# Gated attention and a gelu layer on one core: narrower scores for the last chunk, Strassen products in every batch, and a rearranged start

## The chip, the cores and the metric

The kernel runs on one core of a Trainium2 chip. The metric is the device time of one execution in microseconds (us). A timed run gives one number. The profile is the hardware's record of one execution: for the kernel before it is one more execution beside the timed ones. "Span" is the time from the first to the last instruction of that record; it is some 2 us below the run's device time.

TensorE is PE, its weight loads PEld, VectorE DVE, ScalarE ACT, GpSimd POOL, SyncE SP. PSUM is the memory in which PE leaves its results; ACT or DVE must copy a bank of it out ("drain" it) before PE may use it again.

## The reference, cut to what matters

```python
# u, v: 8 x 3008 x 256, z: 8 x 3008 x 64
scores = (1 / S) * z @ z.T                    # per batch, S = 3008
attn   = maximum(scores, 0) ** 2
x      = u * (attn @ v)                       # 24064 x 256
h      = x @ w_in                             # 256 x 2048
g      = h / (1 + exp(-1.702 * h))
out    = g @ w_out                            # 2048 x 256
```

## The kernel before: the parts that matter

A batch has 3008 rows: five chunks of 512 queries and a last one of 448. 3008 is 23 blocks of 128 and one of 64, and those 64 rows stand twice in the last key block (partitions 0-63 and 64-127). A score unit `(i, jp)` is two key blocks against one chunk of queries. Its two matmuls have 64 rows each and run beside each other in the two halves of the array. ACT then takes the relu, DVE squares it. Because the score matrix is symmetric, squared units of chunk `i` are transposed by DMA (`turn_unit`) and serve later chunks; "turned" units of earlier chunks take over work of the last chunk.

```python
def scores(b, group):                                   # 512 columns always
    ...
        m = CB // 2 if folded(b, i) and jp == 2 * i + 1 else CB
        for r in range(2):
            pe.matmul(sc[:, r, :m * P], zt[h, 2 * kp + r, :],
                      zt[h, (qi + 1) * CB - m:(qi + 1) * CB, :], start=True, stop=True)
```

The second layer's right side `g @ w_out` is made by seven Strassen products (Strassen's method multiplies matrices of 2 x 2 blocks with seven block products, P1 to P7, instead of eight) per chunk of 512 rows (two pairs of row blocks), each product 2 x 8 matmuls of 128 columns. Batches go in pairs: the last chunk of an even batch has 384 rows and that of the odd one 512, which include both 64-row remainders. The 384 rows (three blocks) were made by plain matmuls of 256 columns:

```python
def down(b, k, s):                                      # even batches, last chunk, s = 0, 1, 2
    for ff in range(NFF):                               # 16
        pe.matmul(yp[:, s % 2, :], GT[b, k, ff // CB][:, ff % CB, s * P:(s + 1) * P],
                  W2[:, ff, :], ...)                    # 256 columns
```

At the start of batch 0, z comes in six groups of 512 rows. DVE casts each group to 16 bits, twice (two halves of the same tile), PE transposes it, and ACT or DVE copies it from PSUM to `ZT`. V comes in f32 and POOL casts it. Emission order is the order of each engine's queue:

```python
first_z(0, CB, sp); first_z(CB, 2 * CB, act)            # z groups 0, 1
for n0 in (0, VB): load_v(0, n0)                        # V; its second half chunk on ACT's queue
first_z(2 * CB, 4 * CB, act)                            # z groups 2, 3
...
posts = scores(0, [queue.pop(0) for _ in range(2)])
first_cast(2)                                           # DVE: z group 2
for post_ in posts: post_()                             # ACT relu, DVE square of units 0, 1
keep_warm(3); posts = scores(0, [queue.pop(0)]); keep_warm(2)
first_zt(2)()                                           # PE transposes z group 2
posts[0]()                                              # third unit's relu and square
```

## Time and profile before

| | before |
|---|---|
| median of 3 runs | 1193.93 us (1193.65 to 1197.71) |
| profiled run, span | 1192.27 us, 1190.5 us |
| PE, ACT, DVE busy | 99%, 70%, 69% of the span |

From the page: the busy line and the chain of waits.

```profile
PE 1184.3 (99%) x11433; PEld 721.7 (61%) x11433; DVE 823.6 (69%) x1321; ACT 828.5 (70%) x982; POOL 230.9 (19%) x325
...
PE 98%; DVE 1%; DMA 0%; issue 0%; ACT 0%; ACTq 0%
```

PE is the limit: it is on the chain for 98% of the span, so only what PE does, or waits for, counts. From the groups of PE by form (busy time, mean ns of one, idle before it): the scores and the plain products.

```profile
L244 PE MATMUL sc<-ZT 64*128 64x512 f16 x618 | 111.3, 377 | 0.7
...
L542 PE MATMUL yp<-W,gt 128*128 128x256 f16 x192 | 21.6, 273 | 0.0
```

The mean of one (377 ns) is its pipelined length, not its cost. The cost is the distance to the next start. The timeline of the end of an even batch (start in us, length, engine, line, operation) shows it:

```profile
446.75 1.06 PE L486 MATMUL st<-WT,gt 128*128 128x128 f16 x16
447.64 1.06 PE L486 MATMUL st<-W,gt 128*128 128x128 f16 x16
448.54 1.06 PE L486 MATMUL st<-WT,gt 128*128 128x128 f16 x16
449.43 1.06 PE L486 MATMUL st<-W,s 128*128 128x128 f16 x16
450.32 5.40 PE L542 MATMUL yp<-W,gt 128*128 128x256 f16 x48
455.66 0.39 PE L244 MATMUL sc<-ZT 64*128 64x512 f16 x2
```

A product of 16 matmuls of 128 columns takes 0.89 us from start to start, 56 ns each. The 48 plain ones take 5.34 us, of which about 0.1 us is the change of form before the scores.

At the start DVE was the one to look at. The chain of waits in the first 12 us (start, us, what), and two lines of DVE's timeline (in brackets the idle time before and what ended it):

```profile
1.67 5.59 DMA zf<-in_z_dram
7.26 0.02 issue
7.29 0.49 DVE zst L125 x2
7.78 1.62 DVE a L272 x2
```

```profile
7.29 0.49 DVE L125 CAST zst<-zf 128x256 f16<-128x256 f32 x2 [1.34 <-DMA zf<-in_z_dram]
7.70 1.70 DVE L272 TENSOR_TENSOR a<-rl 128x1024 f16<-128x1024 f16 x2
```

DVE stood idle for 1.34 us until z group 2 landed at 7.26 us, cast it, and only then squared the first unit.

### The profile page before, as it was taken

Reading aid. Unit: us, or ns where it says so; the run is one execution under the profiler, and the core shown is the slowest. Engines: PE = TensorE matmul, PEld = TensorE weight load, DVE = VectorE, ACT = ScalarE, POOL = GpSimd, SP = SyncE. Lnnn points to the kernel's source line nnn. Section 1 sums busy time; section 2 is a strip of 40 time slices with the busy share of each in tenths; the row PEclk is TensorE's granted clock in tenths of the full one; section 3 lists DMA queues with packets and bytes.
Section 4 is the critical chain, followed back from the end, with each engine's and each line's share of the span. In section 5 each row is a group of like instructions: output and inputs, shape, how many; then the busy total and the mean of one; then the engine's idle time right before and its main releaser. Section 6 shows DMA issues by size and latency. Waiting matters only on the chain.

```text
span 1190.5 us, 27555 instructions
## 1 busy us (share of the span) xinstructions
PE 1184.3 (99%) x11433; PEld 721.7 (61%) x11433; DVE 823.6 (69%) x1321; ACT 828.5 (70%) x982; POOL 230.9 (19%) x325
## 2 busy tenths in 40 slices
PE   9999999999999999999999999999999999999998
PEld 3446765467654676546765478554775547855577
DVE  7788755777658775577765877558776487664776
ACT  6878865688656886478864787657876578672785
POOL 5243100231012320133101331014200241001000
PEclk9999999999999999999999999999999999999999
DMA  9996667766687667856778458886579755695012
GB/s 226 191 125 111 128 131 136 84 112 134 138 138 78 108 143 146 130 72 101 160 139 135 68 96 158 159 110 90 104 128 171 108 88 109 138 164 97 1 37 72
DMA packets 373037, 141.80 MB, mean 119 GB/s; under 512 B 315440, under 2 KB 366384, under 8 KB 372912
## 3 DMA queue, kind: packets, MB, share of 16 engines
q1 hardware_dynamic: 314784, 97.30, 45.3%
q0 software_dynamic: 57280, 42.03, 22.7%
q8 instruction: 89, 1.46, 0.5%
q10 hardware_dynamic: 848, 0.72, 0.2%
q14 instruction: 36, 0.29, 0.1%
HBM read 60.29 MB, written 24.64 MB: 71 GB/s over the span
## 4 chain that ended last, share of the span: by engine, by line
PE 98%; DVE 1%; DMA 0%; issue 0%; ACT 0%; ACTq 0%
PE o L344 40%; PE hg L385 27%; PE st L486 23%; PE sc L244 6%; PE yp L542 2%; DMA zf<-in_z_dram 0%; DVE a L272 0%; DVE zst L125 0%; DVE ZT L153 0%; ACT rl L258 0%; ACT ZT L151 0%; ACTq L187 0%; DVE y L502 0%; ACTq L111 0%; PE zp L143 0%
## 5 line engine op out<-in xcount | busy, mean ns | idle before, releaser
L393 ACT ACTIVATE gf<-hg 128x1024 f32<-128x1024 f32 (+1 forms) x384 | 385.5, 1004 | 138.1 <-PE hg L385 115.2
L258 ACT ACTIVATE rl<-sc 128x1024 f16<-128x1024 f32 x309 | 303.2, 1027 | 151.8 <-PE sc L244 148.5
L344 PEld LDWEIGHTS <-V 64*128 64x128 f16 (+1 forms) x4052 | 238.2, 94 | 235.8 <-issue 11.9
L385 PE MATMUL hg<-xt,W 128*128 128x512 f16 (+1 forms) x1408 | 354.6, 374 | 0.0
L397 DVE TENSOR_SCALAR gt<-gf 128x1024 f16<-128x1024 f32 (+1 forms) x320 | 222.5, 696 | 136.7 <-ACT gf L393 133.9
L344 PE MATMUL o<-a,V 64*128 64x512 f16 (+3 forms) x2286 | 303.0, 368 | 0.1
L272 DVE TENSOR_TENSOR a<-rl 128x1024 f16<-128x1024 f16 x274 | 189.8, 698 | 154.1 <-ACT rl L258 153.3
L206 POOL DMA_DIRECT2D uq<-in_u_dram x188 | 127.7, 687 | 612.9 <-PE sc L244 329.3
L344 PE MATMUL o<-tt,V 64*128 64x512 f16 (+1 forms) x1510 | 234.3, 377 | 0.0
L385 PEld LDWEIGHTS <-W 128*128 128x128 f16 x1536 | 139.3, 98 | 119.2 <-issue 2.6
L486 PEld LDWEIGHTS <-gt 128*128 128x128 f16 x2816 | 169.5, 98 | 31.9
L486 PEld LDWEIGHTS <-s 128*128 128x128 f16 x2112 | 127.8, 98 | 25.4 <-issue 0.3
L244 PE MATMUL sc<-ZT 64*128 64x512 f16 (+1 forms) x688 | 121.0, 366 | 0.7
L486 PE MATMUL st<-WT,gt 128*128 128x128 f16 x1408 | 93.0, 219 | 0.0
L486 PE MATMUL st<-WT,s 128*128 128x128 f16 x1408 | 92.3, 219 | 0.0
L486 PE MATMUL st<-W,gt 128*128 128x128 f16 x1408 | 92.3, 219 | 0.0
L502 DVE SCALAR_TENSOR_TENSOR y<-st,uP 128x256 f32<-128x256 f32 x132 | 54.9, 418 | 21.6 <-PE st L486 10.9
L395 ACT ACTIVATE gt<-gf 128x1024 f16<-128x1024 f32 (+1 forms) x64 | 65.9, 1030 | 2.1
L361 DVE TENSOR_TENSOR xt<-o,ut 128x512 f16<-128x512 f32 x80 | 51.3, 683 | 22.7 <-PE o L344 22.7
L244 PEld LDWEIGHTS <-ZT 64*128 64x128 f16 x688 | 38.9, 94 | 44.9 <-issue 9.7
L496 ACT ACTIVATE uP<-st 128x256 f32<-128x256 f32 x132 | 49.6, 376 | 23.2 <-PE st L486 11.2
L459 DVE TENSOR_TENSOR s<-s,gt 128x1024 f16<-128x1024 f16 x88 | 61.5, 699 | 1.0
(54 smaller groups left out, 620.9 us busy)
## 6 DMA issues: line engine op xcount, KB each, us to landing
out_dram<-y SPq DMA_DIRECT2D x40, 512.0 KB, 3.3
uq<-in_u_dram POOLq DMA_DIRECT2D x156, 128.0 KB, 3.7
V<-in_v_dram POOLq DMA_DIRECT2D x35, 256.0 KB, 6.6
tt<-a SPq DMA_TRANSPOSE x232, 3.7
uq<-in_u_dram POOLq DMA_DIRECT2D x32, 112.0 KB, 5.2
vst<-in_v_dram SPq DMA_DIRECT2D x4, 512.0 KB, 6.4
out_dram<-y POOLq DMA_DIRECT2D x4, 384.0 KB, 3.1
zst<-in_z_dram POOLq DMA_DIRECT2D x7, 192.0 KB, 8.4
```

The costliest lines, as they stand in the source:

```text
L206: eng.dma_start(uq[k * QW:(k + 1) * QW, :n // QW].rearrange("t q c k -> t q (c k)"), src[:, :, cs])
L244: pe.matmul(sc[:, r, :m * P], zt[h, 2 * kp + r, :], zt[h, (qi + 1) * CB - m:(qi + 1) * CB, :], start=True, stop=True,)
L258: act.activation(rl, sc, AF.Relu, scale=csc)
L272: dve.tensor_tensor(a, rl, rl, ALU.mult)
L344: ins = pe.matmul(acc[c][:, :n], V16[b][h, j].rearrange("p (c k) -> p k c", k=NCC)[:, c], weights(b, i, j)[h], start=(k, m) == first[c], s ...
L385: pe.matmul(hg[:, e, :n], W1[:, c, ff * P:(ff + 1) * P], XT[b, i][:, c, :n], start=(c == 0), stop=(c == NCC - 1),)
L393: act.activation(gf[:, :, :n], hg[:, :, :n], AF.Gelu_apprx_sigmoid, scale=1.0 / FSC)
L395: act.activation(g, gf[:, :, :n], AF.Copy, scale=FSC)
L397: dve.tensor_scalar(g, gf[:, :, :n], FSC, None, ALU.mult)
L459: dve.tensor_tensor(s_, ST[b, k, "S1", h], a11, ALU.subtract)
L486: pe.matmul(bank[:, m, :], lhs()[:, f, m, :], right[:, ff, :], start=name in ("P1", "P2", "P5") and m == 0 and ff == 0, stop=ff == NFF // ...
L502: dve.scalar_tensor_tensor(y[:, :, o, c], ST[b, k, "bank" + x], 1.0 / FSC, ST[b, k, "after" + u_], ALU.mult, ALU.add,)
```

## The change

Four parts: (1) scores whose queries are the last chunk have 448 instead of 512 columns, and a small extra square fills the repeated 64 columns of the turned units; (2) of the three row blocks that even batches left to plain matmuls, two become Strassen products of 8 matmuls and the third stays plain; (3) in batch 0 the first square no longer stands behind the cast of z group 2, whose transposition moves into the first steps; later casts come earlier; (4) batch 0's DMA transposes are issued in order of use.

```diff
@@ scores, square
-            m = CB // 2 if folded(b, i) and jp == 2 * i + 1 else CB
+            q0, q1 = qi * CH, qi * CH + width(qi)          # width: 448 in the last chunk
+            if folded(b, i) and jp == 2 * i + 1:
+                q0 += CH // 2
-                    sc[:, r, :m * P], ..., zt[h, (qi + 1) * CB - m:(qi + 1) * CB, :],
+                    sc[:, r, :q1 - q0], ..., zt[h].rearrange("d n p -> d (n p)")[:, q0:q1],
-        dve.tensor_tensor(a, rl, rl, ALU.mult)
+        dve.tensor_tensor(a[:, :, :n], rl[:, :, :n], rl[:, :, :n], ALU.mult)
+        if turn:
+            twice = rl[:, :, LFULL:LAST]
+            dve.tensor_tensor(a[:, :, LAST:], twice, twice, ALU.mult)
+            elif b == 0 and jp < NU - 2:                   # transposes in ORDER0
+                squared.setdefault((i, jp // 2), []).append(lambda: turn_unit(b, i, jp, a))
+                while ORDER0 and len(squared.get(ORDER0[0], ())) == 2:
+                    ...
@@ products of the second layer (each sum, copy and output cut to [:, :pairs(b, k)])
+        for k in range(NCH):
             one = [(k, "P6"), (k, "P5"), (k, "P7"), (k, "P2")]
+            if blocks(b)[k][1] < CH:
+                one.insert(0, (k, "odd"))                  # 16 plain matmuls of 256 columns
             lst += [(k, "P1")] + ([(k - 1, "P4"), (k - 1, "P3")] if k else []) + one
@@ start of batch 0
-    FIRST_ZT, FIRST_CAST = {11: 3, 20: 4, 29: 5}, {2: 3, 15: 4, 24: 5}
+    FIRST_ZT, FIRST_CAST = {2: 2, 11: 3, 19: 4, 28: 5}, {2: 3, 8: 4, 16: 5}
+    posts[0]()
     first_cast(2)
-    for post_ in posts:
-        post_()
+    posts[1]()
...
-    first_zt(2)()
-    posts[0]()
...
+                if (b, i, n) == (0, 0, 2):
+                    posts[0]()
```

More of the change, by code (lines that the diff above doesn't have):

```diff
@@ L244, in scores @@
                 pe.matmul(
-                    sc[:, r, :m * P], zt[h, 2 * kp + r, :], zt[h, (qi + 1) * CB - m:(qi + 1) * CB, :],
+                    sc[:, r, :q1 - q0], zt[h, 2 * kp + r, :], zt[h].rearrange("d n p -> d (n p)")[:, q0:q1],
                     start=True, stop=True,
@@ L257, in square @@
             return
-        act.activation(rl, sc, AF.Relu, scale=csc)
+        turn = turned(b, i) and jp >= NU - 2
+        n = width(NCH - 1 if turn else i)
+        act.activation(rl[:, :, :n], sc[:, :, :n], AF.Relu, scale=csc)
         if folded(b, i) and jp == 2 * i:
@@ L275, in square @@
                 late.append(((jp + 2) % NU, lambda: turn_unit(b, i, jp, a)))
+            elif b == 0 and jp < NU - 2:
+                squared.setdefault((i, jp // 2), []).append(lambda: turn_unit(b, i, jp, a))
+                while ORDER0 and len(squared.get(ORDER0[0], ())) == 2:
+                    for turn_it in squared.pop(ORDER0.pop(0)):
+                        turn_it()
             else:
                 turn_unit(b, i, jp, a)
+    ORDER0 = [(0, 1), (0, 2), (1, 2), (0, 3), (1, 3), (0, 4), (2, 3), (1, 4), (2, 4), (3, 4)]
+    squared = {}
     def turn_unit(b, i, jp, a):
@@ L399, in up_group, with pairs @@
             s_()
-        if k < nst(b) and fg in (NFG - 3, NFG - 1):
+        if fg in (NFG - 3, NFG - 1):
             SUMS.extend(left_sums(b, k, fg == NFG - 1))
-    def nst(b):
-        return NCH - 1 + b % 2
+    def pairs(b, k):
+        return blocks(b)[k][1] // (2 * P)
     SUMS, ST = [], {}
@@ L439, in left @@
         g = GT[b, k, h].rearrange("p f (m o t) -> p f m o t", o=2, t=P)
-        return g[:, :, :, odd, :]
+        return g[:, :, :pairs(b, k), odd, :]
     def left_sums(b, k, last):
@@ L454, in left_sum @@
             return
-        s_ = ST[b, k, name, h] = pa.tile([P, CB, 2, P], F16, name="s", tag="a", bufs=26)
+        s_ = pa.tile([P, CB, 2, P], F16, name="s", tag="a", bufs=26)
+        s_ = ST[b, k, name, h] = s_[:, :, :pairs(b, k)]
         if name == "S1":
@@ L461, in left_sum, with products, odd_block @@
             dve.tensor_tensor(s_, a12, ST[b, k, "S2", h], ALU.subtract)
-    def products(n):
+    def products(b):
         lst = []
-        for k in range(n):
+        for k in range(NCH):
             one = [(k, "P6"), (k, "P5"), (k, "P7"), (k, "P2")]
+            if blocks(b)[k][1] < CH:
+                one.insert(0, (k, "odd"))
             lst += [(k, "P1")] + ([(k - 1, "P4"), (k - 1, "P3")] if k else []) + one
-        return lst + [(n - 1, "P4"), (n - 1, "P3")]
+        return lst + [(k, "P4"), (k, "P3")]
+    def odd_block(b, k):
+        s = blocks(b)[k][1] // P - 1
+        yp = ps1.tile([P, D], F32, name="yp", tag="ps1")
+        for ff in range(NFF):
+            pe.matmul(
+                yp, GT[b, k, ff // CB][:, ff % CB, s * P:(s + 1) * P], W2[:, ff, :],
+                start=ff == 0, stop=ff == NFF - 1,
+            )
+        act.activation(Y[b, k][:, s, :], yp, AF.Copy, scale=1.0 / FSC)
     def product(b, k, name):
+        if name == "odd":
+            odd_block(b, k)
+            return
+        mm = pairs(b, k)
         right = {
@@ L478, in product @@
         bank = ST[b, k, "bank" + {"P6": "P1", "P7": "P1", "P4": "P1", "P3": "P5"}.get(name, name)]
-        for m in range(2):
+        for m in range(mm):
             for ff in range(NFF // 2):
@@ L492, in product @@
             Y[b, k] = pw.tile([P, CB, D], F32, name="y", tag="y")
-        y = Y[b, k].rearrange("p (m o) c -> p m o c", o=2)
+        y = Y[b, k].rearrange("p (m o) c -> p m o c", o=2)[:, :mm]
+        bank = bank[:, :mm]
         if name in ("P1", "P6", "P7"):
-            u_ = ST[b, k, "after" + name] = pw.tile([P, 2, P], F32, name="u" + name, tag="u" + name, bufs=1 + (name != "P1"))
+            u_ = pw.tile([P, 2, P], F32, name="u" + name, tag="u" + name, bufs=1 + (name != "P1"))
+            u_ = ST[b, k, "after" + name] = u_[:, :mm]
             act.activation(u_, bank, AF.Copy, scale=1.0 / FSC)
@@ L502, in product @@
             dve.scalar_tensor_tensor(
-                y[:, :, o, c], ST[b, k, "bank" + x], 1.0 / FSC, ST[b, k, "after" + u_], ALU.mult, ALU.add,
+                y[:, :, o, c], ST[b, k, "bank" + x][:, :mm], 1.0 / FSC, ST[b, k, "after" + u_], ALU.mult, ALU.add,
             )
@@ L533, in store @@
                 )
-    def down(b, k, s):
-        if s % 2 == 0:
-            ST[b, k, "yp"] = ps1.tile([P, 2, D], F32, name="yp", tag="ps1")
-        yp = ST[b, k, "yp"]
-        for ff in range(NFF):
-            pe.matmul(
-                yp[:, s % 2, :], GT[b, k, ff // CB][:, ff % CB, s * P:(s + 1) * P], W2[:, ff, :],
-                start=s % 2 == 0 and ff == 0, stop=ff == NFF - 1, skip_group_check=True,
-            )
-        last = s == blocks(b)[k][1] // P - 1
-        if s == 0:
-            Y[b, k] = pw.tile([P, CB, D], F32, name="y", tag="y")
-        if s % 2 or last:
-            act.activation(Y[b, k][:, s - s % 2:s + 1, :], yp[:, :s % 2 + 1, :], AF.Copy, scale=1.0 / FSC)
-        if last:
-            store(b, k, pool)
     LAGY = 2 * NFG
@@ L647 @@
                     load_u(0, 0)
+                if b == 0 and i == 0 and n in FIRST_ZT:
+                    first_zt(FIRST_ZT[n])()
                 if b == 0 and i == 0 and n in FIRST_CAST:
                     first_cast(FIRST_CAST[n])
-                if b == 0 and i == 0 and n in FIRST_ZT:
-                    first_zt(FIRST_ZT[n])()
                 if (i, n) in turn:
@@ L673 @@
                 load_v(b + 1, n0)
-        prods = products(nst(b))
+        prods = products(b)
         for q in range(head, nup):
@@ L684 @@
         steps = [lambda kp=kp: product(b, *kp) for kp in prods]
-        if nst(b) < NCH:
-            k = NCH - 1
-            steps += [lambda s=s: down(b, k, s) for s in range(blocks(b)[k][1] // P)]
         for step in steps:
```

## The prediction

> **What bounds the kernel now.** TensorE: busy 1184.3 of 1190.5 us (99%) in the page's busy table, DVE 69%, ACT 70%; the chain of waits is 98% PE; clock 1.00. After 30 us the timeline has only single PE stalls of about 0.2 us. So outside the start only fewer TensorE cycles count.
>
> The Trainium skill ("TensorE: Matmul & The Clock Gate", the part on 56 ns) gives a warm matmul as N / 2.4 GHz plus about 2.5 ns. The trace agrees: in the chain 176 matmuls of 128 columns took 9.83 us (55.9 ns each), 48 of 256 took 5.24 us (109.2 ns); in the timeline a pair of 64-row matmuls of 512 columns takes 0.216 us, of 448 columns 0.190 us.
>
> **Terms.**
>
> 1. 448 columns. In every batch 12 score units have the last chunk's queries: 96 of 344. Each saves 64 columns of one pair, 0.0267 us: **-2.6 us**, all on the critical path. ACT saves 0.1 us per unit, DVE gains a small square (0.2 us) in 37 units: off the path.
>
> 2. Strassen for the last chunk of the 4 even batches. Before: 48 x 109.2 ns = 5.24 us. After: 16 x 109.2 (odd block) + 56 x 55.9 = 4.87 us: -0.37 each. But products of 8 matmuls last 0.45 us, and draining a bank (ACT starts 0.2 us after the last matmul issued; 0.27 us for 128 columns, an estimate from 0.60 for 512 and 0.38 for 256) takes 0.5. So P7 (waits for P6's copy across P5) and P4 (P7's copy across P2) should stall about 0.1 us each. Net about -0.25 each: **-1.0 us**. The half-size sums are off the path.
>
> 3. Start of batch 0 (z casts and third z transposition moved). Now DVE stands behind the cast of z group 2, which waits for its DMA until 7.26 us; the first square starts at 7.70 though its input was ready at 7.0, and the first output matmul at 8.44. Later stalls: 0.70 us at 15.7 (cast of group 4), 0.2 us at 13.6 and 19.9 (ACT's z copy behind two relus). After: first output matmul at 7.7-7.8, but four transposes (0.21 us) that filled this idle time come after it, and until 20 us each round of 8 or 9 steps is limited by ACT: 0.43 to its start + 1.94 for two relus + 0.6 for the z copy, about 3 us, against 2.8-2.9 measured. So most of the head start is lost again; the 0.70 stall halves. Net **-0.8 us** (0.3 to 1.6).
>
> 4. DMA transposes in order of use: no matmul waits over 0.2 us for a transposed tile now: **0**.
>
> Sum: 4.4 us off 1193.9: **1189.4 us**, range 1187.3 to 1191.3. Chances: faster by over 2% 0.01, within 2% 0.98, slower 0.01.
>
> **What would show it.** 192 score matmuls 64x448 instead of 64x512, pairs 0.190 us apart; even batches' last chunk 4.9-5.1 us with gaps of about 0.1 us before P7 and P4; first output matmul near 7.8 us; chunk 1's first transposed tiles (25.38 us before) used 0.3-1.6 us earlier; ACT busy down 10 us, without effect; no new PE stall on transposed tiles.
>
> **What would make it wrong.** Drain stalls over 0.2 us each, which cancel item 2; a new wait at the start (the third square queues behind casts of groups 2 and 3 and a z copy on DVE); transposes held back by the prescribed order, late for chunk 2; a faster start that meets the V casts on GpSimd (they end at 17.1 us).

## The result and the profile after

| | before | after |
|---|---|---|
| median (6 runs each) | 1193.69 us | 1190.80 us |
| range | 1191.81 to 1197.71 | 1189.91 to 1194.16 |
| profiled span | 1190.5 us | 1188.2 us |

The six runs of the kernel before include the three above. The ratio is 0.9979, 95% interval 0.9959 to 0.9998. A ratio is the mean time of one kernel's fast runs over that of the other's in the same rounds, so it is not quite the ratio of the medians quoted.

The page after, busy line and chain of waits:

```profile
PE 1181.1 (99%) x11529; PEld 724.2 (61%) x11529; DVE 841.9 (71%) x1437; ACT 822.1 (69%) x994; POOL 227.1 (19%) x321
...
PE 98%; DVE 1%; ACT 1%; issue 0%; DVEq 0%; ACTq 0%
```

The groups of PE by form, which answer to the two lines of before:

```profile
L246 PE MATMUL sc<-ZT 64*128 64x512 f16 x426 | 76.7, 380 | 0.4
...
L246 PE MATMUL sc<-ZT 64*128 64x448 f16 x192 | 32.5, 349 | 0.0
...
L495 PE MATMUL yp<-W,gt 128*128 128x256 f16 x64 | 7.6, 272 | 0.0
```

192 score matmuls are narrower, and 64 plain products remain of 192. The end of the same even batch, timeline of PE:

```profile
450.77 1.80 PE L495 MATMUL yp<-W,gt 128*128 128x256 f16 x15
452.41 1.06 PE L520 MATMUL st<-WT,s 128*128 128x128 f16 x16
453.38 0.61 PE L520 MATMUL st<-WT,gt 128*128 128x128 f16 x8
453.83 0.61 PE L520 MATMUL st<-W,gt 128*128 128x128 f16 x8
454.36 0.61 PE L520 MATMUL st<-WT,gt 128*128 128x128 f16 x8
454.80 0.61 PE L520 MATMUL st<-W,s 128*128 128x128 f16 x8
455.34 0.61 PE L246 MATMUL sc<-ZT 64*128 64x512 f16 x4
```

The first line is the odd block (15 of its 16), the second P6 and P5. P7 starts at 453.38, though 16 x 55.9 ns after 452.41 is 453.30: a gap of 0.08 us. P4 (454.36) comes 0.08 us late as well. These are the two drain waits of the prediction. ACT's copies of P6 and of P7, from the same stretch, end at 453.34 and 454.31 us, 0.04 to 0.05 us before P7 and P4 start:

```profile
453.06 0.28 ACT L532 ACTIVATE uP<-st 128x128 f32<-128x128 f32 x1
...
454.03 0.28 ACT L532 ACTIVATE uP<-st 128x128 f32<-128x128 f32 x1 [0.70 <-PE st L520]
```

The start, timelines of PE and of DVE:

```profile
10.87 0.60 PE L246 MATMUL sc<-ZT 64*128 64x512 f16 x4
12.21 0.81 PE L360 MATMUL o<-a,V 128*128 128x512 f16 x3 [0.74 <-DVE a L276]
...
15.68 1.24 PE L360 MATMUL o<-a,V 128*128 128x512 f16 x5
17.91 0.38 PE L360 MATMUL o<-a,V 128*128 128x512 f16 x1 [0.99 <-DVE a L276]
```

```profile
9.87 1.27 DVE L125 CAST zst<-zf 128x256 f16<-128x256 f32 x2
11.07 1.69 DVE L276 TENSOR_TENSOR a<-rl 128x1024 f16<-128x1024 f16 x2
...
15.53 1.31 DVE L125 CAST zst<-zf 128x256 f16<-128x256 f32 x2
16.76 1.69 DVE L276 TENSOR_TENSOR a<-rl 128x1024 f16<-128x1024 f16 x2
```

PE waits twice for a square, and both times two casts stand before that square in DVE's queue. Measured in the array's own time (start minus start of the matmul before minus its columns) the waits are 0.91 and 1.15 us. Neither was there before.

To tell start from the rest I split every trace at the first matmul on a transposed tile (`o<-tt`, the first of chunk 1). The steady stretch runs from there to the start of the last matmul.

| | first transposed tile | steady stretch |
|---|---|---|
| before | 25.38 us | 1161.35 us |
| after | 26.48 us | 1157.90 us |
| difference | +1.10 | -3.45 |

The steady part gave 3.45 us against 3.6 predicted. The start, which was to give 0.8 us, took 1.1.

### The profile page after: what moved, and what is told of

It is laid out like the page before. It is cut to its first block, busy times and chain, and to the rows that moved or that the text cites. A ratio compares the mean times of both kernels' runs of the same rounds, so it can differ in the third digit from the quotient of the medians.

```text
span 1188.2 us, 27887 instructions
## 1 busy us (share of the span) xinstructions
PE 1181.1 (99%) x11529; PEld 724.2 (61%) x11529; DVE 841.9 (71%) x1437; ACT 822.1 (69%) x994; POOL 227.1 (19%) x321
## 4 chain that ended last, share of the span: by engine, by line
PE 98%; DVE 1%; ACT 1%; issue 0%; DVEq 0%; ACTq 0%
PE o L360 39%; PE hg L401 27%; PE st L520 24%; PE sc L246 6%; PE yp L495 1%; ACT rl L262 0%; PE w L99 0%; DVE a L276 0%; DVE zst L125 0%; ACT ZT L151 0%; DVE ut L213 0%; ACT gf L409 0%; DVE WT L448 0%; DVE WT L449 0%; PE zp L143 0%
## 5 line engine op out<-in xcount | busy, mean ns | idle before, releaser
L262 ACT ACTIVATE rl<-sc 128x1024 f16<-128x1024 f32 (+1 forms) x309 | 294.8, 990 | 160.4 <-PE sc L246 115.0
L276 DVE TENSOR_TENSOR a<-rl 128x1024 f16<-128x1024 f16 (+1 forms) x274 | 182.7, 670 | 129.0 <-ACT rl L262 128.2
L520 PEld LDWEIGHTS <-gt 128*128 128x128 f16 x2944 | 177.1, 98 | 32.2
L520 PEld LDWEIGHTS <-s 128*128 128x128 f16 x2208 | 133.7, 98 | 25.6 <-issue 0.5
L246 PE MATMUL sc<-ZT 64*128 64x512 f16 (+2 forms) x688 | 119.0, 360 | 0.4
L520 PE MATMUL st<-WT,gt 128*128 128x128 f16 x1472 | 97.8, 219 | 0.0
L538 DVE SCALAR_TENSOR_TENSOR y<-st,uP 128x256 f32<-128x256 f32 (+1 forms) x144 | 57.6, 407 | 28.5 <-ACT uP L532 19.9
L532 ACT ACTIVATE uP<-st 128x256 f32<-128x256 f32 (+1 forms) x144 | 53.0, 368 | 31.6 <-DVE y L538 14.7
L476 DVE TENSOR_TENSOR s<-s,gt 128x1024 f16<-128x1024 f16 (+1 forms) x96 | 64.9, 676 | 1.1
L474 DVE TENSOR_TENSOR s<-gt 128x1024 f16<-128x1024 f16 (+1 forms) x96 | 64.6, 673 | 0.0
```

The costliest lines, as they stand in the source:

```text
L246: pe.matmul(sc[:, r, :q1 - q0], zt[h, 2 * kp + r, :], zt[h].rearrange("d n p -> d (n p)")[:, q0:q1], start=True, stop=True,)
L262: act.activation(rl[:, :, :n], sc[:, :, :n], AF.Relu, scale=csc)
L276: dve.tensor_tensor(a[:, :, :n], rl[:, :, :n], rl[:, :, :n], ALU.mult)
L474: dve.tensor_tensor(s_, a21, a22, ALU.add)
L476: dve.tensor_tensor(s_, ST[b, k, "S1", h], a11, ALU.subtract)
L520: pe.matmul(bank[:, m, :], lhs()[:, f, m, :], right[:, ff, :], start=name in ("P1", "P2", "P5") and m == 0 and ff == 0, stop=ff == NFF // ...
```

## The experiments

Theory 1: the new order of DVE's queue is bad and costs the start 1.1 us. Theory 2: the two profiled starts are not alike by chance. In the profile before, z group 2 landed at 7.26 us and PE's clock was full from 5.7 us; in the one after, at 8.24 and 7.2 us. One hint stood in the table before the prediction was made: the profiled run, 1192.27 us, was faster than all three timed ones.

### A second look, the old start alone, the order alone, one cast

`after_again` is the changed kernel itself.

> The changed kernel unchanged, for a second look at its start. Theory 1 (the order of DVE's queue costs the start 1.0 us: two stalls of PE on a square, 0.91 us at 12.2 and 1.15 us at 17.9): the two stalls come back, 0.6 us or more each, and the first matmul on a transposed tile is again about 1 us later than in the kernel before (26.48 against 25.38 us). Theory 2 (chance: in the first profile the clock came to full speed at 7.2 instead of 5.7 us and z group 2 landed at 8.2 instead of 7.3): with another phase of the clock the first transposed tile is used at about 25 us, and the stalls are gone or halved. Steady part as in the first profile: 0.36 us less per batch in attention, even tails 0.16 us shorter.

`old_start` undoes parts 3 and 4.

```diff
-    posts[0]()
     first_cast(2)
-    posts[1]()
+    for post_ in posts:
+        post_()
... (all of the start, and ORDER0, as in the kernel before)
```

> The change without its two start parts: z casts, third z transposition, third unit's square and transposes in batch 0 all as before; 448 columns and Strassen kept. Theory 1: about 1 us faster than the changed kernel, 3.4 us faster than the kernel before (ratio about 0.997), stalls at the start as in the kernel before (0.7 us at 15.7). Theory 2: the same as the changed kernel within 0.3 us once the moment of the full clock is allowed for.

`order_off` undoes part 4 alone (the `elif` branch with `ORDER0` goes).

> The changed kernel with its new z casts, but batch 0's DMA transposes issued as they are squared, as before. If the order of the transposes matters, a stall of PE on transposed tiles appears in chunks 1 to 3 or the start changes by over 0.2 us; I expect neither: time as the changed kernel, within 0.3 us, and the same two stalls at the start.

`one_cast` makes one DVE instruction of the two casts of a group.

```diff
-        for c in range(2):
-            dst, src = ZT["st"][g // CB][:, m:m + CB, c, :], ZT["f"][g // CB][:, m:m + CB, :]
-            dve.tensor_copy(dst, src)
+        dst, src = ZT["st"][g // CB][:, m:m + CB], ZT["f"][g // CB][:, m:m + CB, :]
+        dve.tensor_copy(dst, src.unsqueeze(2).broadcast_to([P, CB, 2, DQK]))
```

> The changed kernel with each z group cast by one DVE instruction that reads its source twice (512 elements per partition) in place of two of 256. Theory 1: DVE's queue is the limit at the start and a cast beside GpSimd's casts of V takes 0.65 instead of 0.25 us because it waits for GpSimd's instruction; one instruction per group then saves 0.3 to 0.6 us for each of groups 3 to 5, the stalls at 12.2 and 17.9 us shrink to about half, and the first transposed tile is used 0.6 to 1.2 us earlier. Theory 2: no change at the start beyond the clock's phase.

The kernel before had a median of 1194.22 us (7 runs) beside these. All four are correct, four runs each. These runs were on chip 7; the record does not say on which chip the first two profiles were taken.

| | median | ratio (95%) | z group 2 landed | full clock from | first transposed tile | steady stretch |
|---|---|---|---|---|---|---|
| before, first profile | 1193.93 | | 7.26 | 5.7 | 25.38 | 1161.35 |
| after, first profile | 1190.80 | 0.9979 | 8.24 | 7.2 | 26.48 | 1157.90 |
| after_again | 1190.41 | 0.9967 (0.9946 to 0.9989) | 8.37 | 4.7 | 26.61 | 1157.77 |
| old_start | 1191.13 | 0.9976 (0.9952 to 1.0001) | 7.98 | 4.5 | 26.51 | 1157.87 |
| order_off | 1190.12 | 0.9977 (0.9941 to 1.0014) | 8.14 | 6.4 | 26.37 | 1157.86 |
| one_cast | 1189.45 | 0.9954 (0.9929 to 0.9979) | 8.02 | 5.4 | 25.57 | 1159.70 |

Landings are those of the DMA that brings groups 2 and 3, and all but the medians and ratios come from the traces. From DVE's timelines, the cast of z group 2 in `old_start` and in `after_again` (in brackets DVE's wait for the landing):

```profile
8.00 0.49 DVE L125 CAST zst<-zf 128x256 f16<-128x256 f32 x2 [2.25 <-DMA zf<-in_z_dram]
```

```profile
8.40 0.91 DVE L125 CAST zst<-zf 128x256 f16<-128x256 f32 x2 [0.82 <-DMA zf<-in_z_dram]
```

The old start in `old_start` is no better than the new one: 26.51 us, with the same order of instructions at the start as in the kernel before. So the 25.38 us that I predicted from was a lucky look, and theory 1 falls as an explanation of the 1.1 us: undoing the change doesn't bring them back. Theory 2 holds for the difference between the two profiles. The clock is only part of it: `after_again` had the full clock 2.5 us earlier and was no faster.

But the two stalls on squares did come back in `after_again` (0.5 and 0.9 us; before them PE stood 1.27 us at the third z transposition, as z landed late), and `one_cast`, which only shortens DVE's queue, uses the first transposed tile about 0.9 us earlier than its siblings at about the same landing. Its two stalls on squares were 0.83 and 0.60 us, where `order_off`, with the same order of casts, had 0.90 and 0.90; so they shrank, but not to half as was expected, and its clock was also full 1 us earlier than that of `order_off`. DVE's queue is thus one limit of the new start, as far as one trace can show it. The old one came to the same time by other waits: in `old_start` PE stood 0.99 us at the third z transposition, as z landed, 0.54 us at a square and 0.90 us at the transposition of group 4, behind its two casts.

A cast of 256 elements took about 0.25 us (half of a pair's 0.49) while POOL was idle and about 0.65 us beside POOL's casts of V; the single cast of 512 took 0.43 alone and 0.79 to 0.83 beside them, against 1.27 to 1.31 for a pair. From DVE's timeline in `one_cast`:

```profile
10.01 0.79 DVE L124 CAST zst<-zf 128x512 f16<-128x512 f32 x1
```

The Trainium skill ("SBUF — State Buffer", the section on its two separate sides) says that a DVE instruction of a two-port mode, or one with two inputs in SBUF, and a GpSimd instruction take a shared pair of ports as an exclusive lock for a whole instruction. No run shows in which mode the casts ran, but the traces agree with a wait for the end of POOL's instruction: in the 14 profiles every cast of z that started while a cast of V was running on POOL ended a fixed time after that cast of V, 0.14 to 0.15 us for 256 elements (41 of 41) and 0.28 us for 512 (16 of 16). So one instruction waits once, two can wait twice. The squares were stretched too, from 0.69 to as much as 1.10 us, while POOL cast V.

`one_cast` lost its profiled gain again elsewhere, in the profiled run only. The waits of PE between 60 and 80 us:

```profile
PE hg L400 <- DMA W<-in_moe_w_in_dram: 1.6, 2, 1.3
```

The first weights came late: the slowest of their four loads took 13.4 us to land, against 6.8 us at most in the profile before and 8.8 in the one after. Its other three spans were 1187.0 to 1187.7 us, against 1188.2, 1188.2 and 1188.3 for the lowest three of `after_again`.

The order of the DMA transposes shows nothing in the trace of `order_off`: the split and the stretch are those of the two profiles of the changed kernel within about 0.2 us, and the two stalls on squares (0.90 us each) are there. But one of its four runs took 1198.03 us, at a mean clock of 0.997, the longest of any changed kernel here. It has no trace, so its cause is open.

### The two steady parts alone, and two tries at the start

`cols_only` is the kernel before with part 1, `strassen_only` with part 2.

> The kernel before with the 448 columns alone. Prediction: 12 x 0.0267 = 0.32 us less per batch, 2.6 us in all; attention of each later batch 0.32 us shorter in the trace, ffn and tails unchanged. If the extra small square on DVE or anything else gave some back, less. Its start is a further look at the start of the kernel before: first transposed tile used at about 26.5 us if the first profile of before (25.38) was a lucky one, at about 25.4 us if not.

> The kernel before with the Strassen pair of the even batches alone. Prediction: 0.37 us less in each of 4 tails minus two drain stalls of 0.08 us: 0.21 us each, 0.8 us in all; attention unchanged. Rival: tails in the changed kernel gained only because of the narrower scores beside them; then the tails here gain less. Start: as for the columns alone, a further look at the start of before.

`z_first` moves a load of V behind z:

```diff
     first_z(2 * CB, 4 * CB, act)
-    load_v(0, 2 * VB)
     first_z(4 * CB, NJ, sp)
+    load_v(0, 2 * VB)
```

> The changed kernel with the third chunk of V (rows for j 8 to 11) issued after all of z instead of before its last third. If the landing of z group 2 (8.2 us in most looks, 7.3 in the first profile of before) bounds the start, it lands 0.5 to 1.5 us earlier here, the stalls behind it shrink and the first transposed tile is used 0.3 to 1 us before the changed kernel's 26.5 us. Rival: DVE's queue and ACT bound the start whatever z does; then the time stays within 0.2 us.

`one_cast_w_early` is `one_cast` with the first weights loaded earlier:

```diff
-    LOADW = {(3, 16): 0, (3, 24): 1, (3, 32): 2, (3, 40): 3, ...
+    LOADW = {(2, 44): 0, (3, 4): 1, (3, 12): 2, (3, 20): 3, ...
```

> One cast per z group, and the four loads of the first weights issued 20 steps earlier in batch 0. In the profile of the single cast PE waited 0.46 and 1.47 us for these weights (68 and 73 us), which no other profile shows. If such late weights make the slower runs (1190 us and more of span), here no run has them: spans within 1187.0 to 1188.0 us, median about 1189 us; start about 0.9 us better than the changed kernel. Rival: slower runs have another cause and stay.

The kernel before: 1193.86 us (8 runs; seven of them are those of the rounds above).

| | median | ratio (95%) | z group 2 landed | first transposed tile | steady stretch |
|---|---|---|---|---|---|
| cols_only | 1190.42 | 0.9962 (0.9937 to 0.9987) | 7.96 | 26.94 | 1158.61 |
| strassen_only | 1192.81 | 0.9979 (0.9953 to 1.0005) | 9.19 | 28.74 | 1160.53 |
| z_first | 1190.24 | 0.9963 (0.9942 to 0.9984) | 7.78 | 26.47 | 1157.77 |
| one_cast_w_early | 1189.74 | 0.9956 (0.9935 to 0.9978) | 9.60 | 26.50 | 1157.76 |

The steady stretch of `cols_only` is 2.74 us shorter than before (predicted 2.6; the rest is not traced), that of `strassen_only` 0.82 us (predicted 1.0); the sum, 3.56 us, is what the whole change shows (3.45 and 3.58 in its two profiles). In `strassen_only` each even tail was 0.15 to 0.16 us shorter up to the start of the last matmul, and 0.05 us more came after it, because a matmul of 128 columns is last instead of one of 256. The attention of the later batches was otherwise unchanged. The rival for the tails falls. A part that I did not foresee: with the narrower columns one wait at the head of batch 0's Strassen products (about 100 us) is 0.13 us longer; why, I did not find out.

Both kernels have the old start, and both show how it depends on z. In `strassen_only` z group 2 landed at 9.19 us. PE's timeline and two of its windows (us, then busy time of PE, PEld, DVE, ACT and POOL with instructions, granted clock, DMA share, GB/s):

```profile
6.90 0.60 PE L99 MATMUL w<-nil 128*128 128x512 f16 x2
10.31 0.40 PE L143 MATMUL zp<-ident,zst 128*128 128x128 f16 x4 [2.81 <-DVE zst L125]
10.90 1.01 PE L348 MATMUL o<-a,V 128*128 128x512 f16 x2 [0.19 <-DVE a L272]
```

```profile
8.00:12.00 4.00, 1.49 (x8) 0.49 (x8) 2.79 (x5) 0.36 (x1) 2.82 (x4) 0.84 0.99 298
12.00:16.00 4.00, 4.00 (x18) 1.31 (x17) 2.90 (x5) 1.94 (x3) 3.67 (x6) 0.73 1.00 254
```

PE and DVE both stood in line behind that landing. After the wait the clock was at half for 3.41 us (10.75 to 14.16 us in the trace), and with a landing 1.2 us later than in `old_start` the first transposed tile came 2.2 us later. The old start has four looks, 25.4, 26.5, 26.9 and 28.7 us, in the order of the landing but for a tie at 8.0. The new start (`after`, `after_again`, `order_off` and, with another order of V, `z_first`) has 26.4 to 26.6 us, with landings of 7.8 to 8.4. With one cast a landing as late as 9.60 us gave 26.50 us; the 0.9 us expected of `one_cast_w_early` did not show. All this is one profile for each kernel: the order by landing is what the looks show, not a rule.

`z_first` missed: z group 2 landed at 7.78 us, hardly sooner. The early weights (the last of their loads issued at 55.6 instead of 60.6 us) leave the trace without a wait on them, although one took 11.7 us to land; but spans of 1186.6 to 1188.4 us are no narrower than I can tell from chance with four runs.

### z ahead of V on ACT's queue

Groups 2 and 3 of z are issued from ACT's queue behind 256 KB of V. `early_z` is `one_cast_w_early` with these two in the other order:

```diff
+    first_z(2 * CB, 4 * CB, act)
     for n0 in (0, VB):
         load_v(0, n0)
-    first_z(2 * CB, 4 * CB, act)
```

> The single cast and the early weights, and on ACT's DMA queue z groups 2 and 3 ahead of the second half of V's first chunk (one swap of lines). In ten looks z group 2 landed at 7.3 to 9.6 us, behind 256 KB of V on the same queue; here it should land at about 5.5 to 6.5 us, and V's rows for j 2 and 3 at about 7.5 instead of 5.3. If the landing of z is what moves the start between runs, the stall at the third z transposition (0.2 to 1.5 us) goes and the first transposed tile is used at about 25.5 us or earlier, with less scatter of the spans. Rival (DVE and ACT bound the start): no gain over the single cast, about 25.6 us.

`early_z_sched` uses the earlier landing:

```diff
-    posts[0]()
-    first_cast(2)
-    posts[1]()
+    for g in (2, 3):
+        first_cast(g)
+    for post_ in posts:
+        post_()
... (first_zt(2) and the third unit's square before the steps again)
-    FIRST_ZT, FIRST_CAST = {2: 2, 11: 3, 19: 4, 28: 5}, {2: 3, 8: 4, 16: 5}
+    FIRST_ZT, FIRST_CAST = {4: 3, 12: 4, 20: 5}, {5: 4, 10: 5}
```

> As early_z, and with z there early the emission is rearranged: casts of groups 2 and 3 before the first square, third z transposition in PE's idle time before the first output matmul, groups 3 to 5 transposed 7 to 8 steps earlier, so that ACT's z copy comes before and not behind two relus. If DVE's queue order and ACT's chain of 3 us per round bound the start, the rounds of 8 or 9 steps between score groups shrink from about 3 to 2.5-2.7 us, the first transposed tile is used at 24 to 25 us, and the spans fall to about 1185.5 to 1187 us, the fastest of all kernels here. If z45, which lands at 10 to 11.5 us, is not there when its cast comes to the head of DVE's queue, a stall on a square of 0.5 to 1 us shows instead.

The kernel before: 1194.06 us (7 runs).

| | median (4 runs) | ratio (95%) | spans | z group 2 landed | first transposed tile |
|---|---|---|---|---|---|
| early_z | 1188.86 | 0.9959 (0.9942 to 0.9976) | 1186.7 to 1187.4 | 5.05 | 24.80 |
| early_z_sched | 1187.76 | 0.9951 (0.9936 to 0.9966) | 1185.8 to 1186.7 | 5.14 | 23.76 |

The swap alone brings the landing from 7.3-9.6 us (ten profiles) to 5.05 us here and to 5.1-5.5 us in the three kernels below that keep it; the 256 KB of V that now come second land at 8.2 to 8.7 us instead. These rounds ran on another chip (1, the last ones 13) than the earlier ones (7). The Trainium skill ("DMA: Bandwidth & Descriptors", the section on queues, rings and completion order) says that each DMA engine consumes a queue's descriptors in ring order and goes round between queues; it fits that the place within the queue counted and that moving V on the other queue (`z_first`) hardly did.

With the rearranged emission the first transposed tile is used 2.7 us sooner than in the changed kernel's first profile. DVE and PE in `early_z_sched`, lines of their timelines:

```profile
5.76 0.75 DVE L124 CAST zst<-zf 128x512 f16<-128x512 f32 x2
6.88 0.69 DVE L275 TENSOR_TENSOR a<-rl 128x1024 f16<-128x1024 f16 x1 [0.37 <-ACT rl L261]
7.79 0.69 DVE L275 TENSOR_TENSOR a<-rl 128x1024 f16<-128x1024 f16 x1 [0.22 <-ACT rl L261]
```

```profile
10.36 0.60 PE L245 MATMUL sc<-ZT 64*128 64x512 f16 x4
...
12.96 0.61 PE L245 MATMUL sc<-ZT 64*128 64x512 f16 x4
...
15.77 0.61 PE L245 MATMUL sc<-ZT 64*128 64x512 f16 x4
...
18.31 0.39 PE L245 MATMUL sc<-ZT 64*128 64x512 f16 x2
```

Both casts fit in the time in which DVE has nothing else, and the rounds from one score group to the next take 2.5 to 2.8 us, where the changed kernel took 3.4 and 4.0 us (10.87, 14.26, 18.21).

### The drain of the short products, and the order once more

`best_products` is `early_z_sched` with other work in the drain times:

```diff
-                one.insert(0, (k, "odd"))
+                one = [(k, "P6"), (k, "P2"), (k, "P5"), (k, "P7"), (k, "odd")]
```

> As early_z_sched, with the order of the last even chunk's products changed from odd, P6, P5, P7, P2, P4, P3 to P6, P2, P5, P7, odd, P4, P3. If the two gaps of 0.08 us before P7 and P4 are drain waits (the copy of a bank takes longer than one product of 8 matmuls), 0.9 us of other work now stands before P7 and 1.75 us before P4: both gaps go, each even tail is 0.16 us shorter, 0.65 us in all, spans about 1185.2 to 1185.5 us. Rival: the gaps belong to something else about these products and move with them.

> As early_z_sched, with batch 0's DMA transposes issued as they are squared instead of in order of use. With the start some 2.5 us faster the transposed tiles are needed sooner; if the order protects anything, PE stalls on transposed tiles of chunks 2 or 3 (30 to 65 us) by 0.3 us or more appear here. If the order is worth nothing, as with the slower start, the trace is the same within 0.2 us.

The kernel before: 1193.62 us (7 runs).

| | median (4 runs) | ratio (95%) | spans | first transposed tile | steady stretch |
|---|---|---|---|---|---|
| best_products | 1187.01 | 0.9939 (0.9918 to 0.9959) | 1184.9 to 1185.5 | 24.38 | 1157.15 |
| best_order_off | 1187.85 | 0.9963 (0.9920 to 1.0007) | 1185.3 to 1193.7 | 24.44 | 1157.99 |

The end of the same even batch in `best_products`, timeline of PE:

```profile
450.74 1.36 PE L494 MATMUL yp<-W,gt 128*128 128x256 f16 x11
451.94 0.61 PE L519 MATMUL st<-WT,gt 128*128 128x128 f16 x8
452.39 0.61 PE L519 MATMUL st<-W,s 128*128 128x128 f16 x8
452.93 0.61 PE L245 MATMUL sc<-ZT 64*128 64x512 f16 x4
```

The odd block runs straight into P4 and P3; both gaps are gone (P7, at 449.75 us, also starts 0.45 us after P5, as without a wait), and each even tail is 0.16 us shorter than in `early_z_sched`, 0.66 us over the stretch (1157.15 against 1157.81), as expected. The start is 0.6 us later here, on another chip; the clock was full from 5.9 instead of 4.7 us, and the 0.6 us that half of this difference makes would account for it, which no run tests.

`best_order_off` shows no wait on transposed tiles in chunks 2 and 3, so in its trace the order of the DMA transposes is worth nothing there either. In `early_z`, which has the order, PE waited once for a transposed tile (about 0.5 us at 73 us); so late tiles are possible with it. One run of `best_order_off` was long (1195.5 us, span 1193.7, mean clock 0.997); it has no trace, and its cause is open. Of the kernels with a new start, the two without the order thus had one such run in four each, and those with it none in 34 runs (longest 1194.16 us). The kernel before, without the order too, had some up to 1198.49 us. This may be chance, but it leaves open whether the order protects against something rare.

`best_products` is correct and the fastest here: 6.6 us below the kernel before in the medians, where the change itself gave 2.9 to 3.8 (in other rounds; the two did not run side by side).

## Why the prediction was right or wrong

The time, 1190.80 us against 1189.4, lies in the range, and most of the sum was right.

- **PE is the limit and ACT's relief is worth nothing: right.** ACT was busy 6.4 us less (10 predicted) and the steady stretch shows PE's terms alone.
- **448 columns, 2.6 us: right.** 2.74 us measured by itself. Exactly 192 matmuls became narrower.
- **Strassen, 0.25 us per even batch after two drain waits of about 0.1 us: right.** 0.21 us each; the two waits were 0.083 and 0.081 us, and filling them with other products gave back 0.16 us per tail. The skill page "TensorE: Matmul & The Clock Gate" (the part on 56 ns) and the trace agree on what a matmul costs, so these two terms could be added up from counts.
- **Start, 0.8 us: the step that failed.** The prediction took one start, that of the profile, as the start of the kernel, and it was an unusual one: z group 2 landed at 7.26 us, the earliest of the looks with that queue. Three further looks at the old start gave 26.5 to 28.7 us for the first transposed tile instead of 25.38. With a like landing (about 8 us) the new start gains little or nothing: 26.4 to 26.6 us against 26.5 and 26.9. What it gains with a late landing is not shown, as none of its looks had one. In the medians of the same rounds `after_again` is 0.7 us below `old_start`, with four runs each; how much the start gains on average stays open within some such figure. The head start itself was there: at like landings the first output matmul came at 7.7 to 8.4 us in the new start and at 9.2 and 10.0 us in the old one (`old_start`, `cols_only`). It was lost again by the first transposed tile, as the prediction said of most of it, and the stalls on squares are the longest waits in between besides those for z. The detail was wrong too: the 0.70 us stall did not halve. It turned into two stalls on squares, of 0.9 and 1.15 us, behind casts in DVE's queue, the first of which the prediction named among the things that would make it wrong.
- **First output matmul at 7.7-7.8 us: in the second look only** (7.67 us). In the first it came at 8.37 us, with the clock at half until 7.2 us, and in `order_off` and `z_first` at 8.06 us.
- **Order of the DMA transposes, 0: right** as far as the traces of two comparisons show; two long runs without a trace stay open.
- **What the profiles differ by.** Steady -3.45, start +1.10: -2.35 of the 2.3 us between the spans. The medians differ by 2.9 us in the first rounds and 3.8 us in the second, more than the profiles; that would fit a typical old start slower than the profiled one, but with four to seven runs each it does not show it. The time lies in the range without the start: by an estimate from the two numbers, 1193.7 less the steady 3.45 is 1190.2 us.

## What to carry to other kernels

Where one engine is busy 99% of the time, count its instructions by form and price each by the distance between starts: terms of 0.2 us in 1190 then come out right. Don't take the fill of a pipeline from a single profile: look at whether the profiled run is a typical one, find the DMA landing on which the start hangs, and make the start bear a late one. First look at the queue order of what lands late (here two lines swapped): moving the instructions that wait for it gained 0.4 to 1.0 us at the start once it landed early, and at most 0.6 us at like landings before.

## What the Trainium skill lacked or had wrong

- "TensorE: Matmul & The Clock Gate" gives an idle window of about 3.4 us before the clock drops, and `strassen_only` agrees: the clock fell at 10.75 us, 3.42 us after the columns of the last ordinary matmul had ended, with 2.97 us of idle time and four transposes in between; no run shows whether the transposes count. Its remark that the moment of the full clock varies by half a us from run to run was too narrow here: that moment lay between 3.9 and 7.2 us of the span in the 14 profiles, with the first matmul at 1.19 us in all of them.
- "SBUF — State Buffer" gives the lock between DVE and GpSimd without its price for short casts: 0.25 us became about 0.65 us (per cast of a pair), a cast of 256 elements ended 0.14 to 0.15 us after the POOL instruction that it met, and two casts of 256 elements cost 1.3 us where one of 512 cost 0.8 us.
- "DMA: Bandwidth & Descriptors" states the order within a queue and the turns between queues, but has no figure for what a place in the queue is worth at the start of a kernel: 256 KB of V ahead of z on one queue moved its landing from 5.1-5.5 to 7.3-9.6 us (four and ten profiles).
- No page that I read says that one profile's start may, beyond the phase of the clock, be far from the typical one: 25.38 us against 26.5 to 28.7 us for the same order of instructions, with z landing at 7.26 us against 8.0 to 9.2 us.
